# Three result transfers move from ScalarE's queue to GpSimd's, and ten blank products open the program in place of fourteen

## The chip, the core and the metric

The kernel runs on one core of one Trainium2 chip. The metric is device microseconds (us) of one execution, and less is better. A core has five engines with a queue of their own each, which run in order: TensorE (PE; its weight loads are listed apart as PEld), VectorE (DVE), ScalarE (ACT), GpSimd (POOL) and SyncE (SP). ACT, POOL and SP also start transfers (DMA). An instruction that waits for a semaphore holds up everything behind it in its queue.

## What is computed

An mLSTM cell over 768 steps for 4 batches x 8 heads of dimension 40, and behind it a feed-forward block with g = h - tanh(h):

```python
def _attn_ref(q, k, v, i_gate, f_gate, o_gate):
    ...
    for t in range(S):
        m_new = np.maximum(f_gate[:, :, t] + m, i_gate[:, :, t])
        f_stab = np.exp(f_gate[:, :, t] + m - m_new)
        i_stab = np.exp(i_gate[:, :, t] - m_new)
        C = f_stab[..., None, None] * C + i_stab[..., None, None] * np.einsum('bhd,bhe->bhde', vt, kt)
        n = f_stab[..., None] * n + i_stab[..., None] * kt
        h_tilde = np.einsum('bhde,bhe->bhd', C, qt)
        denom = np.maximum(np.abs(np.einsum('bhd,bhd->bh', n, qt)[:, :, None]), 1.0)
        y[:, :, t] = h_tilde / denom / (1.0 + np.exp(-o_gate[:, :, t]))

x = attn_out.transpose(0, 2, 1, 3).reshape(3072, 320)
h = x @ w_in                    # 320 x 2048
out = (h - np.tanh(h)) @ w_out  # 2048 x 320
```

## The kernel before

**Tiles.** The sequence is cut into chunks of 128 steps. A unit is one chunk of one batch (24 units), a group is two units, so 256 rows of x (12 groups). The 2048 hidden columns are eight pairs of 256, numbered p = 0 to 7. An item is one or two pairs of one group: it makes h ("up", tile `ph_up`), shrinks it to g (tile `gt`) and multiplies by `w_out` ("down", tiles `po` or `pS`).

**Two phases.** The first six units, the conversion of the weights and the first pairs of groups 0 to 2 are laid out by a small planner (`Plan`, lines 157 to 267). It keeps a time for each engine, and where TensorE would have nothing to do it puts in blank products (`awake`, line 428, or `stream`): matmuls of a constant, whose results nobody reads. `idle` (line 1704) decides how many. From about 107 us on a loop (line 1759) places the rest. There both products of an item are made with seven block products in place of eight, which needs sums of blocks: of x and of w_in (tiles `sums_in` and `part`, made on POOL in `sum_w_in`), of w_out (`wT`, POOL) and of g (`s`, DVE).

**The up product of the second phase** (`up_in_seven`, line 1227) has three stages in two PSUM banks. In stage three the sum lands in bank half b; ACT copies it to e (the last `COPY ph_up<-ph_up` of an item), and only then may PE add the last products to b. In the profile that is the group `ph_up<-xT,w_in` of 20 (4 of 128x128 and 16 quarters). Behind it PE has the attention products of a unit (`pT`, `pc`) and the down products of the item before (`pS`). DVE then adds (`both`), cubes and multiplies (`gt`), and PE's first up product of the next item has to wait until the cubes have read the banks.

**Groups 0 to 2.** Their first pairs were done in the planned phase and their sums lie in `part0` to `part2` in SBUF. Their last four pairs are done as two items each at the start of the loop, groups 0, 1, 2 in turn. When the last of them is done, `put_together` (line 1073) gathers the banks into the tile `ob` on DVE; later on DVE `add_parts` (line 1092) adds the stored sums, and `ob` is sent to `out`. The tile `part0` to `part2` is used again behind that: `sum_w_in` writes block sums of w_in for p = 0, 1, 2 into it on POOL.

**What sets the order.** Each engine's instructions are pinned in the order in which the code is run. `Clock.later(key, wait, step)` (line 141) puts a step off until an estimated clock has moved on by `wait`: `add_parts` comes 6.0 behind the gathering, and the transfer 1.0 behind `add_parts`. Whatever the loop emits in between stands between them on its engine.

Of the kernel before, what the change touches and what calls it, by code (L numbers as in the profile page):

```python
# [79 lines left out]
def kernel(  # L80
# [33 lines left out]
    V, A, SP, G = Pinned(nc.vector), Pinned(nc.scalar), Pinned(nc.sync), Pinned(nc.gpsimd)  # L114
# [42 lines left out]
    class Plan:  # L157
# [45 lines left out]
        def flow(cls, moved):  # L203
# [22 lines left out]
            return ends  # L226

        def run(self, idle, fill):
            while self.todo:
                ready = [(t, op) for op in self.todo if (t := self.start(op)) is not None]  # L230
# [23 lines left out]
                if op["engine"] == "T":  # L254
                    n = idle(self.free["T"], t)
                    self.done.append((t - n, t, 1.0))
                    us = us * (self.COLD[1] if t < self.COLD[0] else 1.0) + self.TURN * (op["tiles"] != self.tiles)
                    self.tiles = op["tiles"]
                    self.done.append((t, t + us, op["dense"]))
# [168 lines left out]
    def awake(n):  # L428

        if not spare:  # L430
            spare.append(ps_o.tile([128, 512], FP, name="awake", tag="po1"))
        stream(spare[0], n)

    def stream(bank, n):
        for _ in range(n):
            T.matmul(bank.rearrange("p (h t) -> p h t", h=HH), diag[:, 0], diag[:, 0:1].to_broadcast([128, HH, L]), start=True, stop=True)
# [636 lines left out]
    def put_together(g):  # L1073
        bank = pS[g]

        ob = mlp.tile([128, 5, HM], FP, name="ob", tag="ob")
        a = mlp.tile([128, HM], FP, name="a", tag="a", bufs=1)
        u = mlp.tile([128, 2, HM], FP, name="u", tag="u", bufs=1)

        def twice(t):  # L1080
            return t.unsqueeze(1).to_broadcast([128, 2, HM])

        def rest():
            V.tensor_tensor(out=ob[:, 0:5:4], in0=bank[0][:, 0:2], in1=twice(a), op=OP.add)
            V.tensor_tensor(out=u, in0=bank[1], in1=twice(ob[:, 4]), op=OP.add)
            V.tensor_tensor(out=ob[:, 3], in0=bank[1][:, 0], in1=u[:, 1], op=OP.add)
            V.tensor_tensor(out=ob[:, 1:3], in0=bank[2], in1=u, op=OP.add)
            c, b = divmod(g * GT, B)
            rows = out.rearrange("(b c t) n -> c t b n", b=B, c=NT)[c][:, b:b + GT]
            whole = ob[:, 0:4].rearrange("p (t two) n -> p t (two n)", two=2)  # L1090

            def add_parts():
                both = ob[:, 0:2 * GT]
                V.tensor_tensor(out=both, in0=both, in1=parts_of[g].rearrange("p t (two n) -> p (t two) n", two=2), op=OP.add)
                Clock.later("sent", 1.0, lambda: A.dma_start(out=rows, in_=whole))

            if g < FIRST:
                Clock.later("sent", 6.0, add_parts)
            else:
                Clock.later("sent", 2.0, lambda: A.dma_start(out=rows, in_=whole))  # L1100

        if g in third:
            return lambda: A.copy(out=a, in_=bank[0][:, 2]), rest
        A.copy(out=a, in_=bank[0][:, 2])
        Clock.later("result", 0.5, rest)
# [321 lines left out]
    plan = Plan(small=("b0", "b1"), a=1, up=1, po0=1, po1=1, gt=2, z=1, s4=1, P=4, vs=4, w64a=2, w64b=2, w=2, wm=2, ob=2)  # L1427
# [45 lines left out]
    of_tokens, of_states, exponentials, rows = {}, {}, [], []  # L1473
# [230 lines left out]
    def idle(t0, t1, share=0.9):  # L1704


        one = 0.43 if t0 < plan.COLD[0] else 0.217
        n = int((t1 - t0) * (1.0 if t0 < plan.COLD[0] else share if t0 > 18.0 or share == 1.0 else 0.65) / one)
        if n and not busy:
            awake(n + 4 if t0 < plan.COLD[0] else n)  # L1710
        else:
            pool, tag = next(((pool, tag) for name, pool, tag in (("a", ps_a, "a0"), ("up", ps_h, "ph0"), ("po0", ps_o, "po0"), ("po1", ps_o, "po1"))
                              if plan.tokens[name] and plan.tokens[name][0][0] <= t0), (None, None))
            if n and pool:
                stream(pool.tile([128, 512], FP, name="awake", tag=tag), n)
            else:
                n = 0
        return n * one

    plan.run(idle, lambda t0, t1: idle(t0, max(t1, t0 + 0.25), 1.0))  # L1720


# [280 lines left out]
```

## Time and profile before

| | |
|---|---|
| median of 3 runs | 495.69 us (495.55 to 496.15) |
| profiled execution, its own time | 496.64 us |
| profiled execution, span from first to last instruction | 494.9 us |
| mean granted clock of TensorE | 0.994 |
| PE idle in the whole span | 11.4 us (494.9 less 483.5 busy) |
| transfers `out<-ob` of 320 KB, started by ACT | 11, issue 0.36 to 0.44 us each |

The page gives the busy time of each engine, the share of each in the chain of work that ended last, and groups of instructions by tile. Times in the rows of the timeline are start and length; "[x <-Y]" behind a row says that the engine was idle for x us before it, and what ended that by the profile. Where TensorE is busy nearly all the time, its few idle stretches are the place to look.

### The profile page before, as it was taken

Reading aid. Unit: us, or ns where it says so; the run is one execution under the profiler, and the core shown is the slowest. Engines: PE = TensorE matmul, PEld = TensorE weight load, DVE = VectorE, ACT = ScalarE, POOL = GpSimd, SP = SyncE. Lnnn points to the kernel's source line nnn. Section 1 sums busy time; section 2 is a strip of 40 time slices with the busy share of each in tenths; the row PEclk is TensorE's granted clock in tenths of the full one; section 3 lists DMA queues with packets and bytes.
Section 4 is the critical chain, followed back from the end, with each engine's and each line's share of the span. In section 5 each row is a group of like instructions: output and inputs, shape, how many; then the busy total and the mean of one; then the engine's idle time right before and its main releaser. Section 6 shows DMA issues by size and latency. Waiting matters only on the chain.

```text
span 494.9 us, 13827 instructions
## 1 busy us (share of the span) xinstructions
PE 483.5 (98%) x5212; PEld 434.8 (88%) x5212; DVE 411.6 (83%) x966; ACT 268.9 (54%) x729; POOL 125.7 (25%) x248
## 2 busy tenths in 40 slices
PE   9999999999899989999999999999999999999995
PEld 5778877789798989999999999999999999898985
DVE  4899989998988988888888888888887988885853
ACT  4888978544344544554554454464455464454540
POOL 5642325826431522102112102102102102102000
PEclk9999999999989999999999999999999999999998
DMA  7995485223634435345445354454344343320001
GB/s 226 294 259 187 75 164 159 74 50 89 141 81 118 81 94 126 77 106 109 96 107 110 75 120 103 81 124 101 66 115 103 65 115 60 59 56 17 28 2 32
DMA packets 140076, 51.26 MB, mean 104 GB/s; under 512 B 119908, under 2 KB 132388, under 8 KB 140004
## 3 DMA queue, kind: packets, MB, share of 16 engines
q1 hardware_dynamic: 131084, 31.18, 30.8%
q0 software_dynamic: 5440, 15.05, 10.7%
q10 hardware_dynamic: 3480, 4.10, 2.4%
q8 instruction: 43, 0.70, 0.6%
q14 instruction: 29, 0.24, 0.2%
HBM read 38.40 MB, written 11.60 MB: 101 GB/s over the span
## 4 chain that ended last, share of the span: by engine, by line
PE 88%; DVE 4%; DMA 2%; SPq 1%; ACT 1%; issue 1%; POOL 0%; ACTq 0%; DVEq 0%
PE ph_up L129 38%; PE pS L129 30%; PE po L129 5%; PE pT L129 4%; PE ps L129 3%; PE pc L129 2%; PE awake L129 2%; PE ph L129 2%; SPq L106 1%; DMA z_in<-h_rows 1%; DVE gt L106 1%; DVE s L106 1%; DMA h_rows<-zt 1%; DVE ob L106 1%; ACT z L106 1%
## 5 line engine op out<-in xcount | busy, mean ns | idle before, releaser
L129 PE MATMUL ph_up<-xT,w_in 64*64 64x256 f32 (+3 forms) x1324 | 155.7, 350 | 4.4 <-ACT ph_up L106 3.3
L129 PEld LDWEIGHTS ph_up<-xT,w_in 128*128 128x128 f32 (+2 forms) x1324 | 114.1, 162 | 22.0 <-issue 4.7
L106 ACT COPY ph_up<-ph_up 128x256 f32<-128x256 f32 x117 | 41.8, 357 | 100.6 <-PE ph_up L129 60.5
L106 ACT ACTIVATE z<-ph_up 128x256 f32<-128x256 f32 (+1 forms) x98 | 40.6, 416 | 93.0 <-PE ph_up L129 88.4
L106 POOL DMA_DIRECT2D xT<-y_rows x54 | 31.6, 590 | 224.5 <-DMA y_rows<-yt 205.6
L129 PE MATMUL pS<-wT,s 128*128 128x160 f32 x504 | 86.7, 300 | 0.0
L129 PEld LDWEIGHTS pS<-wT,s 128*128 128x128 f32 x504 | 72.9, 191 | 0.3 <-issue 0.3
L106 ACT ACTIVATE q<-z,tiny 128x512 f32<-128x512 f32 (+1 forms) x98 | 68.9, 713 | 2.5
L106 DVE SCALAR_TENSOR_TENSOR gt<-q,gt 128x512 f32<-128x512 f32 (+1 forms) x98 | 66.0, 681 | 3.7 <-ACT q L106 1.1
L106 DVE TENSOR_TENSOR both<-ph_up,cs 128x256 f32<-128x256 f32 x78 | 32.7, 423 | 36.0 <-PE ph_up L129 31.4
L129 PE MATMUL pS<-w_out,gt 128*128 128x160 f32 x336 | 56.9, 312 | 0.0
L129 PE MATMUL ph_up<-xT,sums_in 128*128 128x128 f32 x336 | 51.6, 276 | 0.5 <-DVE gt L106 0.5
L129 PEld LDWEIGHTS pS<-w_out,gt 128*128 128x128 f32 x336 | 46.8, 190 | 4.4 <-issue 1.9
L129 PEld LDWEIGHTS ph_up<-xT,sums_in 128*128 128x128 f32 x336 | 45.5, 191 | 1.3 <-issue 0.7
L129 PE MATMUL ph_up<-xT,part 128*128 128x128 f32 x288 | 44.8, 278 | 0.0
L106 DVE SCALAR_TENSOR_TENSOR gt<-ph_up,z 128x256 f32<-128x256 f32 (+1 forms) x98 | 41.2, 459 | 2.3 <-ACT z L106 2.2
L129 PEld LDWEIGHTS ph_up<-xT,part 128*128 128x128 f32 x288 | 38.9, 191 | 1.7 <-ACT ph_up L106 1.7
L106 DVE TENSOR_TENSOR s<-gt 128x256 f32<-128x256 f32 x84 | 32.8, 431 | 1.4
L129 PE MATMUL pS<-wT,gt 128*128 128x160 f32 x168 | 29.8, 300 | 0.0
L129 PE MATMUL pS<-w_out,s 128*128 128x160 f32 x168 | 29.7, 299 | 0.0
L129 PE MATMUL po<-w_out,gt 128*128 128x320 f32 x96 | 27.9, 439 | 0.0
L106 DVE SCALAR_TENSOR_TENSOR gt<-both,z 128x512 f32<-128x512 f32 x39 | 27.0, 692 | 0.0
(141 smaller groups left out, 745.7 us busy)
## 6 DMA issues: line engine op xcount, KB each, us to landing
w<-in_moe_w_out POOLq DMA_DIRECT2D x8, 640.0 KB, 5.9
h_rows<-zt SPq DMA_DIRECT2D x68, 64.0 KB
z_in<-h_rows SPq DMA_DIRECT2D x68, 64.0 KB
w<-in_moe_w_in POOLq DMA_DIRECT2D x16, 256.0 KB, 6.0
kz<-in_kT SPq DMA_DIRECT2D x48, 80.0 KB
o<-in_o_gate SPq DMA_DIRECT2D x24, 160.0 KB
qz<-in_qT SPq DMA_DIRECT2D x44, 80.0 KB
out<-ob ACTq DMA_DIRECT2D x11, 320.0 KB
```

What stands on the lines that cost most here:

```text
L106: i = method(*args, **kwargs)
L129: return cls.keep(nc.tensor.matmul(*args, **kwargs))
```

## The change

Two lines are edited:

```diff
             def add_parts():
                 both = ob[:, 0:2 * GT]
                 V.tensor_tensor(out=both, in0=both, in1=parts_of[g].rearrange("p t (two n) -> p (t two) n", two=2), op=OP.add)
-                Clock.later("sent", 1.0, lambda: A.dma_start(out=rows, in_=whole))
+                G.dma_start(out=rows, in_=whole)
...
         if n and not busy:
-            awake(n + 4 if t0 < plan.COLD[0] else n)
+            awake(n)
```

The transfers of groups 0, 1 and 2 are started by POOL, and no longer put off. The planner's numbers are as they were; the first call of `awake` now makes 10 blank products, and the four that go are the last four ahead of the first transposes on PE (`gate<-ident,w_in`). No other instruction of PE, DVE or SP changes its place.

On ACT, in the item behind the end of group 0 (`cs` is a copy of half a bank, `z` and `q` are the first steps of the shrinking), these rows stood:

```order
144 L106 COPY ph_up<-ph_up 128x256
145 L106 COPY cs<-ph_up 128x256
146 L106 COPY ph_up<-ph_up 128x256
147 L106 DMA out<-ob 128x2x320
148 L106 COPY ph_up<-ph_up 128x256
```

and now these:

```order
144 L106 COPY ph_up<-ph_up 128x256
145 L106 COPY cs<-ph_up 128x256
146 L106 COPY ph_up<-ph_up 128x256 x2
147 L106 ACTIVATE z,sums<-ph_up 128x256 x2
148 L106 ACTIVATE q<-z,tiny 128x512
```

The transfer stood ahead of the last copy of the item, the one that lets PE go on; now nothing stands between the two copies. The same holds at the ends of groups 1 and 2.

On POOL, at the same place, the rows now are (`part_145` is the tile of group 0's sums, used again for w_in's; `xT` is x of a later group, fetched through `y_rows` in DRAM):

```order
83 L106 MEMSET k 128x40
84 L106 MEMSET vs 128x23
85 L106 DMA out<-ob 128x2x320
86 L106 TENSOR_TENSOR part_145<-w_in 128x2x128
87 L106 TENSOR_TENSOR part_145<-w_in,part_145 128x128 x2
88 L106 DMA xT_90<-y_rows 64x3x128
```

Row 85 is new, and the rest has moved down by one. Row 86 had to wait for the same addition on DVE before, since it overwrites the tile that the addition reads. At group 2 it is:

```order
110 L106 TENSOR_TENSOR wT<-w_out 128x160
111 L106 TENSOR_TENSOR wT<-w_out,wT 128x160
112 L106 DMA out<-ob 128x2x320
113 L106 TENSOR_TENSOR part_147<-w_in 128x2x128
114 L106 TENSOR_TENSOR part_147<-w_in,part_147 128x128 x2
115 L106 DMA xT_91<-y_rows 64x3x128
```

Again only the transfer (row 112) is new.

## The prediction

> **What bounds the kernel.** I read the page's busy times first, then the list of who waited for whom on PE.
>
> ```profile
> PE 483.5 (98%) x5212; PEld 434.8 (88%) x5212; DVE 411.6 (83%) x966; ACT 268.9 (54%) x729; POOL 125.7 (25%) x248
> PE 88%; DVE 4%; DMA 2%; SPq 1%; ACT 1%; issue 1%; POOL 0%; ACTq 0%; DVEq 0%
> PE ph_up L129 <- ACT ph_up L106: 3.3, 2, 1.8
> PE ph_up L129 <- POOL part L106: 1.0, 1, 1.0
> ```
>
> PE is busy for 98% of the span and makes 88% of the chain that ended last. The two lines of waits (us in total, times, longest) are three gaps of 4.3 us together, and no other line of that list behind PE's start has more than 0.5. So the time is PE's work plus these few gaps, and the question is which gaps go. The timeline shows the first of the three, at the end of group 0:
>
> ```profile
> 133.11 0.61 PE L129 MATMUL ph_up<-xT,w_in 128*128 128x128 f32 x4
> 133.56 0.61 PE L129 MATMUL ph_up<-xT,sums_in 128*128 128x128 f32 x4
> 134.18 0.82 DVE L106 TENSOR_TENSOR ob<-ob,part 128x640 f32<-128x640 f32 x1
> 135.03 0.44 ACTq L106 DMA_DIRECT2D out<-ob  x1
> 135.51 0.36 ACT L106 COPY ph_up<-ph_up 128x256 f32<-128x256 f32 x1 [3.06 <-DVE o L106]
> 135.92 2.15 PE L129 MATMUL ph_up<-xT,w_in 128*128 128x128 f32 x20 [1.76 <-ACT ph_up L106]
> ```
>
> Read from below: PE waits for ACT's copy, the copy stands behind the issue of the transfer, and the issue behind DVE's addition, which ends at 135.00. ACT itself had been idle for 3.06 us. The other two are alike:
>
> ```profile
> 156.06 0.61 PE L129 MATMUL ph_up<-xT,part 128*128 128x128 f32 x4
> 157.22 0.36 ACT L106 COPY ph_up<-ph_up 128x256 f32<-128x256 f32 x1 [2.26 <-DVE o L106]
> 157.72 1.71 PE L129 MATMUL ph_up<-xT,w_in 128*128 128x128 f32 x20 [1.05 <-POOL part L106]
> ...
> 176.23 0.61 PE L129 MATMUL ph_up<-xT,sums_in 128*128 128x128 f32 x4
> 178.41 1.74 PE L129 MATMUL ph_up<-xT,w_in 128*128 128x128 f32 x20 [1.57 <-ACT ph_up L106]
> ```
>
> The second is put down to POOL's `part`. I take it for a coincidence: these products read no `part` tile, and ACT's copy ends 0.14 us ahead of them, at 157.58.
>
> **The change, part by part. 1. The transfers leave ACT.** The copy then needs only PE's product that stands two groups ahead, so it is done before PE asks for it. Groups of four such products follow each other in 0.45 us (133.11 to 133.56), so PE's 20 products could start at 133.56 + 0.45 = 134.01 and not 135.92: 1.91 us. At the second place it is 157.72 - 156.51 = 1.21, at the third 178.41 - 176.68 = 1.73. Together 4.85.
>
> The first gap cost more than its length:
>
> ```profile
> 137.00:138.00 1.00, 1.00 (x18) 0.56 0.06 16
> 138.00:139.00 1.00, 1.00 (x28) 0.50 0.27 40
> 139.00:140.00 1.00, 1.00 (x32) 0.50 0.24 38
> 180.00:181.00 1.00, 1.00 (x48) 1.00 0.23 39
> 140.89 1.35 PE L129 MATMUL pS<-w_out,gt 128*128 128x160 f32 x8
> 161.06 1.35 PE L129 MATMUL pS<-w_out,gt 128*128 128x160 f32 x8
> ```
>
> The column behind PE's busy time is the granted clock. It falls to half at 137 behind the first gap, for some 3 us, and stays at 1.00 behind the third. From the 20 products to the next `pS` PE takes 140.89 - 135.92 = 4.97 us there, and 161.06 - 157.72 = 3.34 at the second place: 1.6 us lost. Without the gap this goes too. PE's lead at 140.89 is then 1.91 + 1.6 = 3.5 us.
>
> The Trainium skill, TensorE: Matmul & The Clock Gate, "What's actually happening", says that the clock is halved after a window of about 3.4 us with too little work, and that the windows run free of the kernel. The trace agrees with the length; by that rule the 1.6 us would be in some executions and not in others, which is the first rival below.
>
> **2. What DVE takes back.** PE cannot keep the whole lead, since DVE is nearly full in this stretch. DVE gains only where it was idle for want of PE:
>
> ```profile
> 138.17 0.96 DVE L106 TENSOR_TENSOR both<-ph_up,cs 128x256 f32<-128x256 f32 x2 [0.90 <-PE ph_up L129]
> 146.44 0.49 DVE L106 TENSOR_TENSOR ob<-pS,a 128x320 f32<-128x320 f32 x1 [0.49 <-ACT a L106]
> 149.37 0.42 DVE L106 TENSOR_TENSOR both<-ph_up,cs 128x256 f32<-128x256 f32 x1 [0.76 <-PE ph_up L129]
> 150.32 0.75 DVE L106 SCALAR_TENSOR_TENSOR gt<-ph_up,z 128x256 f32<-128x256 f32 x2
> 152.20 0.61 PE L129 MATMUL ph_up<-xT,part 128*128 128x128 f32 x4
> 159.54 0.96 DVE L106 TENSOR_TENSOR both<-ph_up,cs 128x256 f32<-128x256 f32 x2 [0.55 <-PE ph_up L129]
> 171.15 0.74 DVE L106 SCALAR_TENSOR_TENSOR gt<-ph_up,z 128x256 f32<-128x256 f32 x2
> 172.37 0.61 PE L129 MATMUL ph_up<-xT,sums_in 128*128 128x128 f32 x4
> 190.11 0.96 DVE L106 TENSOR_TENSOR both<-ph_up,cs 128x256 f32<-128x256 f32 x2 [1.32 <-PE ph_up L129]
> ```
>
> The rule is that PE's first up product of an item comes behind the two cubes (`gt<-ph_up,z`) of the item before. DVE's lead by 150.32 is 0.90 + 0.49 + 0.76, say 2.1. The cubes then end at 151.07 - 2.1 = 148.97, and PE, which with its 3.5 would be there at 148.70, starts at 149.0: its lead falls to 3.2. The second place adds 1.21: 4.4. DVE has 2.1 + 0.55 = 2.65 by then. In the item that ends group 2 the cubes end at 171.89 - 2.65 = 169.24, and PE would be there at 172.37 - 4.4 = 167.97. It waits 1.3 us, and its lead falls to 3.1. The third place adds 1.73: **4.8 us**. Behind it DVE gains 1.32 more at 190.11, and the groups from 3 on have no additions of parts, so I let nothing be lost there.
>
> Bounds for this term: if DVE gained nothing at all before 172.37, PE's lead there could be 172.37 - 171.89 = 0.5, and with 1.73 it ends at 2.2. If DVE took nothing back it would be 4.85 + 1.6 = 6.45. The 4.8 follows the rows step by step, so I take it.
>
> **3. The issue on POOL.** The trace has no transfer of `ob` by POOL; the nearest are others that POOL starts:
>
> ```profile
> L106 POOL DMA_DIRECT2D xT<-y_rows x54: 534/612/642, 131.1 to 445.5; - x54
> L106 POOL DMA_DIRECT2D w<-in_moe_w_out x8: 722/736/751, 7.8 to 78.9; - x8
> 177.69 0.84 POOL L106 TENSOR_TENSOR part<-w_in 128x256 f32<-128x256 f32 x1 [7.48 <-DVE ob L106]
> 178.60 1.05 POOL L106 TENSOR_TENSOR part<-w_in,part 128x128 f32<-128x128 f32 x2
> 184.05 0.61 PE L129 MATMUL ph_up<-xT,part 128*128 128x128 f32 x4
> ```
>
> An issue takes 0.53 to 0.75 us of POOL; I take 0.74, from the one with the same shape of rows (128x2x320). POOL waited for the same addition before, so no wait is new, and `part` comes 0.74 later. Queued behind are `part` and the `xT` transfers, which wait for `y_rows` anyway. The tightest user is the last: PE reads group 2's `part` at 184.05, with its lead at 179.25. POOL's wait for the addition would end at 177.69 - 2.65 = 175.0, and it is done with issue and sums (177.69 to 179.65, so 0.74 + 1.96) at 177.7. So 1.5 us are left and the cost is nothing; without that cover it would be up to 0.74.
>
> **4. Four blank products fewer.**
>
> ```profile
> 4.05 1.18 PEld L129 LDWEIGHTS <-diag 128*128 128x128 bf16 x6 [0.23 <-issue]
> 5.05 0.41 DVE L106 TENSOR_TENSOR w_out<-w_out,w_in 32x256 f32<-32x256 f32 x1
> 5.66 0.20 PEld L133 LDWEIGHTS gate<-ident,w_in 32*128 32x128 f32 x2 [0.42 <-issue]
> 21.91 0.49 DVE L106 TENSOR_SCALAR w_e<-w 128x640 int32<-128x640 int32 x1 [0.40 <-DMA w<-in_moe_w_in]
> ```
>
> The fast ones follow each other in 1.18 / 6 = 0.2 us, so PE is free 0.8 us earlier. But the second transposes need DVE's row of 5.05, which ends at 5.46, so the work behind them gains some 0.2 (5.66 less 5.46). At 21.91 DVE waits for the weights' transfer, which no PE work starts, and a lead from the start ends there. I take 0. Ends: -0.8 if all of it survived; +1.6 if PE, now idle for some 0.4 us and then on short products, lost the clock once as it did at 137.
>
> **The sum.** 4.8 + 0 + 0 off the profiled execution's 496.64 gives **491.8 us**. The median, 495.69, lies 0.95 under the profiled execution. Two readings: the recording costs that, and the timed runs lose the clock as well, then it is 495.69 - 4.8 = 490.9; or they don't lose it. In that case the old program would reach the second place 1.6 us sooner, with DVE as sooner, so the gain is 4.8 - 1.6 = 3.2 and the time 492.5. 491.8 lies between them and I keep it.
>
> **The rivals.**
> - *No clock loss in the timed runs*: 492.5, as just worked out. For it speaks that the second and third gap (1.05 and 1.57 us) show none, so 1.76 is near the edge. It lies inside my forecast, which I give as 490.6 to 493.2: 0.74.
> - *DVE holds PE throughout*: a lead of 2.2 or less, 493.4 to 494.5. For it: DVE is idle at little more than the rows shown, and the units' transfers through DRAM could arrive no sooner. Against it: the third gap stands behind the last gathering, and goes whole. 0.13.
> - *The clock at the start*: 1.6 us on top, 492.5 to 494.1. For it: ahead of 5.46 PE would have little but two short transposes. Against it: at 178.41 PE had been idle for 1.57 us and kept its clock. 0.08.
> - *The edit does nothing* (PE waits for `part` at all three places, as the profile writes at the second): 495.7. Against it: the tiles that these products read. 0.03.
> - *Slower*: POOL's issue is long. If the third one took 0.74 + 1.5 = 2.2 us, PE would start to wait for `part` at 184.05; with the lead of 4.8 it would be slower beyond 7.0 us an issue. All 54 + 8 issues above lie under 0.76, against it. 0.02, 496.5 and above.
>
> The Trainium skill, DMA: Bandwidth & Descriptors, "SWDGE vs HWDGE vs iDMA", speaks against the change: plain transfers belong to SP or ACT, since GpSimd computes its descriptors in software and DVE can lock it out of the memory that it writes them to. By that rule POOL's issue could stretch as in the last rival; the issue rows above, made beside a busy DVE, show nothing of it.
>
> **How the numbers follow.** The range 490.6 to 493.5 takes in both readings and most of the start's bound. A measurement of this kernel can tell about 0.2% (1.0 us) from no change. Faster by more than that: the forecast, the start and nearly all of the second rival, 0.93; within it 0.05; slower 0.02.
>
> **What would show it.** In the profile after, the 20 products at the three places have no wait for ACT; the granted clock stays at 1.00 there; PE has new waits for DVE's `gt` near 149 and 167 to 169, some 1.6 us together; POOL's three issues take about 0.74 each. I am wrong if PE waits for `part`, if the clock falls between 5 and 12 us, or if the gaps go and come back whole as waits for DVE behind 180.

## The result, and the profile after

| | before | changed |
|---|---|---|
| median, 20 runs each | 495.98 us | 491.52 us |
| lowest to highest | 494.94 to 497.81 us | 491.00 to 497.14 us |
| mean | 495.99 us | 493.21 us |

The ratio of the times is 0.9944, with a 95% interval from 0.9917 to 0.997. The prediction, 491.8 us with a range from 490.6 to 493.5, holds the median. It does not hold the runs: they lie in two clusters, 13 from 491.0 to 491.8 and 7 from 496.4 to 497.1, with nothing between. The upper cluster was not foreseen at this price: its rival, "the clock at the start", had 492.5 to 494.1. The profiled execution, at 496.5 us, is one of the seven, so its profile shows both what the change gained and what it lost.

First lines of the page and, from the list of who waited for whom on PE, two lines of the kernel after (us in total, times, longest):

```profile
span 494.8 us, 13817 instructions
PE 486.8 (98%) x5208; PEld 435.5 (88%) x5208; DVE 411.2 (83%) x966; ACT 268.9 (54%) x729; POOL 127.2 (26%) x251
PE ph_up L129 <- DVE gt L106: 1.3, 3, 0.7
PE pS L129 <- DVE ob L106: 0.3, 1, 0.3
```

The two lines of before that made 4.3 us (waits for ACT's copy and, by the list, for POOL's `part`) are gone. Yet the span is that of before, 494.8 against 494.9, and PE is busy for 486.8 us where it was 483.5, with four instructions fewer. PE took longer for the same work somewhere. The timeline at the end of group 0 shows the gain:

```profile
138.13 0.36 ACT L106 COPY ph_up<-ph_up 128x256 f32<-128x256 f32 x1 [0.86 <-PE ph_up L129]
138.37 0.61 PE L129 MATMUL ph_up<-xT,sums_in 128*128 128x128 f32 x4
138.82 1.63 PE L129 MATMUL ph_up<-xT,w_in 128*128 128x128 f32 x20
138.99 0.82 DVE L106 TENSOR_TENSOR ob<-ob,part 128x640 f32<-128x640 f32 x1
140.10 0.74 POOL L106 DMA_DIRECT2D out<-ob  x1 [2.17 <-DVE ob L106]
...
158.33 1.64 PE L129 MATMUL ph_up<-xT,w_in 128*128 128x128 f32 x20
159.55 0.74 POOL L106 DMA_DIRECT2D out<-ob  x1 [7.84 <-DVE ob L106]
160.31 0.92 POOL L106 TENSOR_TENSOR part<-w_in 128x256 f32<-128x256 f32 x1
178.84 0.61 PE L129 MATMUL ph_up<-xT,w_in 128*128 128x128 f32 x4
```

ACT's copy is done by 138.49, ahead of DVE's addition, and the 20 products follow the four before them after 0.45 us. At the second place they start at 158.33, ahead of POOL's `part` at 160.31, so `part` was indeed never what they waited for. But all of this comes late: the group at 138.37 stood at 133.56 before. The timeline of PE's first 19 us shows where the 4.8 us went (three rows of before, then those of after):

```profile
6.02 1.16 PE L129 MATMUL ps<-qz,kz 40*128 40x128 f32 x16
7.59 1.24 PE L129 MATMUL awake<-diag 128*128 128x512 bf16 x5
11.98 1.88 PE L129 MATMUL ph<-vs,P 128*128 128x41 f32 x16
```

```profile
5.52 0.42 PE L133 MATMUL gate<-ident,w_in 32*128 32x32 f32 x2
6.08 2.08 PE L129 MATMUL ps<-qz,kz 40*128 40x128 f32 x16
8.97 2.34 PE L129 MATMUL awake<-diag 128*128 128x512 bf16 x5
13.25 3.86 PE L129 MATMUL awake<-diag 128*128 128x512 bf16 x9
16.94 1.88 PE L129 MATMUL ph<-vs,P 128*128 128x41 f32 x16
```

The same 16 products take 2.08 us and not 1.16, the same 5 blank ones 2.34 and not 1.24, and so on up to 16.8 us. Only the group at 16.94 has its old length. In this execution TensorE never left the half clock with which it starts until then, while before it left it at 4.05 (in the prediction's rows, the six weight loads at 0.2 us). The granted clock is of no help here:

```profile
14.00:16.00 2.00, 2.00 (x6) 0.76 (x5) 0.00 (x0) 1.97 (x5) 1.99 (x4) 1.00 0.73 268
```

This window of after has 1.00 in the column behind the engines' busy times, though the six blank products in it follow each other at 0.43 us, where six of the prediction's rows take 0.2 each. The trace's own record of the clock begins only at the rise, here at 16.82 us, and the column shows 1.00 for the time ahead of it. There the clock has to be told from the distances.

### The profile page after: what moved, and what is told of

The parts are those of the page before. It is cut to its first block, busy times and chain, and to the rows that moved or that the text cites. A ratio compares the mean times of both kernels' runs of the same rounds, so it can differ in the third digit from the quotient of the medians.

```text
span 494.8 us, 13817 instructions
## 1 busy us (share of the span) xinstructions
PE 486.8 (98%) x5208; PEld 435.5 (88%) x5208; DVE 411.2 (83%) x966; ACT 268.9 (54%) x729; POOL 127.2 (26%) x251
## 4 chain that ended last, share of the span: by engine, by line
PE 89%; DVE 6%; issue 1%; ACT 1%; DMA 1%; SPq 1%; DVEq 0%; ACTq 0%
PE ph_up L129 38%; PE pS L129 30%; PE po L129 5%; PE ps L129 4%; PE pT L129 4%; PE awake L129 3%; PE pc L129 2%; PE ph L129 2%; DVE gt L106 1%; DVE s L106 1%; DVE ob L106 1%; SPq L106 1%; ACT z L106 1%; DVE ys L106 1%; DVE zt L106 1%
```

## The experiments

Two theories stood against each other. A: the ten blank products make the clusters, and the transfers gain about 4.6 us in every run. B: the transfers on POOL make the clusters.

**Each part alone, more blank products, and ACT's queue behind the copy.** The four kernels are:

```diff
 e1: transfers on GpSimd, but
+            awake(n + 4 if t0 < plan.COLD[0] else n)
 e2: the kernel before, but
+            awake(n)
 e3: transfers on GpSimd, but
+            awake(n + 8 if t0 < plan.COLD[0] else n)
 e4: the kernel before, but
+                Clock.later("sent", 2.0, lambda: A.dma_start(out=rows, in_=whole))
```

> The transfers on GpSimd, but fourteen blank products at the first as before. Theory A (the changed kernel's two clusters of times come from its ten blank products: where TensorE's clock does not rise during them, it stays low until about 16 us and the program is 5 us late; the transfers themselves are worth 4.6): one cluster near 491.3, no run above 494, and in the profile fast blank products from about 4 us. Rival B (the two clusters come from the transfers on GpSimd): two clusters, 491.3 and 496.5, the upper with about a third of the runs. Rival C (the good cluster of the changed kernel owes something to the earlier start): one cluster at 492 or above.

> The kernel before with ten blank products in place of fourteen; the transfers stay on ScalarE. Theory A: two clusters, about 495.9 with some two thirds of the runs and about 501 with a third. Rival B: one cluster near 495.9. Rival C: a lower cluster clearly under 495.9, by as much as e1 lies above 491.3.

> The transfers on GpSimd and eighteen blank products at the first. Theory A: fourteen are enough, so one cluster; four more fast products of 0.2 us delay the start by 0.8, of which the wait of VectorE for the weights near 22 us should take up most: 491.3 to 492.1. If fourteen are not quite enough (some runs of e1 high), e3 has fewer of these than e1. Rival B: two clusters as in e1.

> The kernel before with its fourteen blank products and the three transfers on ScalarE, put off by 2.0 in place of 1.0, so that each stands behind the copy that lets TensorE go on and not ahead of it. Theory A (only the place ahead of the copy cost time, not ScalarE's queue): the same as e1, about 491.3, and no wait of the twenty products for ScalarE. Rival D (ScalarE's queue itself, its issue or what stands behind the transfer, costs as well, and GpSimd is the gain): 492.5 to 495, with waits for ScalarE left in the profile.

The runs of the kernel before on the same chip had a median of 495.68 (17 runs). All times below are in us; "upper" counts the runs that lie 4 us or more above the others of their kernel.

| | blank products | transfers | median (runs) | lowest to highest | upper | ratio, 95% interval |
|---|---|---|---|---|---|---|
| e1 | 14 | POOL | 491.77 (6) | 491.10 to 493.27 | 0 | 0.9927 (0.9911 to 0.9942) |
| e2 | 10 | ACT, ahead of the copy | 495.13 (12) | 494.41 to 500.06 | 1 | 0.9987 (0.9976 to 0.9998) |
| e3 | 18 | POOL | 492.46 (5) | 492.38 to 493.00 | 0 | 0.9936 (0.9924 to 0.9949) |
| e4 | 14 | ACT, behind the copy | 491.89 (5) | 491.55 to 492.53 | 0 | 0.9928 (0.9916 to 0.9941) |

A holds in all four: the upper cluster comes with ten blank products, with the transfers on either queue. Two of its numbers did not: e2 has 1 run of 12 in the upper cluster where a third was expected, and e1 is spread over 2.2 us. e4 is the same as e1, and its 20 products wait for nothing at the three places, so nothing of the gain is POOL's: it is enough that the transfer no longer stands ahead of the copy. Rival C has a small part of the truth: e2's lower runs, at a median of 495.06, are 0.6 under before. And e3 is 0.7 over e1, so a later start is not taken up by the wait of DVE near 22 us, against what was expected.

e2's profiled execution fell in its upper cluster, like that of after. The two differ by the transfers alone, so PE's timeline in them can be laid side by side. Rows of e2 (the waits have the names that they had before), and the window behind its first gap:

```profile
138.41 0.61 PE L129 MATMUL ph_up<-xT,sums_in 128*128 128x128 f32 x4
140.76 1.52 PE L129 MATMUL ph_up<-xT,w_in 128*128 128x128 f32 x16 [1.75 <-ACT ph_up L106]
158.41 0.61 PE L129 MATMUL ph_up<-xT,part 128*128 128x128 f32 x4
160.96 0.68 PE L129 MATMUL ph_up<-xT,w_in 128*128 128x128 f32 x4 [1.04 <-POOL part L106]
177.31 0.66 PE L129 MATMUL ph_up<-xT,sums_in 128*128 128x128 f32 x4
181.82 0.38 PE L129 MATMUL ph_up<-xT,w_in 128*128 128x128 f32 x1 [1.69 <-ACT ph_up L106]
```

```profile
141.00:145.00 4.00, 4.00 (x90) 3.51 (x90) 3.23 (x10) 2.28 (x8) 0.88 (x2) 1.00 0.34 93
```

and the two of after that are still missing for the pairs:

```profile
156.99 0.61 PE L129 MATMUL ph_up<-xT,part 128*128 128x128 f32 x4
176.13 0.71 PE L129 MATMUL ph_up<-xT,sums_in 128*128 128x128 f32 x4
```

The lead of after over e2 is 0.04 us ahead of the first place (138.41 less 138.37) and 1.94 behind it (140.76 less 138.82); 1.42 ahead of the second and 2.63 behind it; 1.18 ahead of the third and 2.98 behind it. So the places give 1.90, 1.21 and 1.80, and DVE takes back 0.5 and 1.45 between them. In e2 the gap of 1.75 cost no clock, as the window behind it shows (1.00): without that, the transfers are worth 3.0 us at the third place and 3.1 at PE's last product. The spans differ by more, 3.6. Behind PE's last product each of the twelve profiles has another 4.5 to 5.3 us, which do not follow the change (e1 4.5, e4 5.3).

**How many blank products, and who takes the lead back.**

```diff
 e5: the changed kernel, but
+            awake(n - 3 if t0 < plan.COLD[0] else n)
 e6: the changed kernel, but
+            awake(n + 2 if t0 < plan.COLD[0] else n)
 e7: e1, but in add_parts
-                V.tensor_tensor(out=both, in0=both, in1=parts_of[g]...
+                G.tensor_tensor(out=both, in0=both, in1=parts_of[g]...
```

> The changed kernel with seven blank products at the first in place of ten. Theory A (the clock rises at a moment that differs from run to run over some 3.4 us, seen at 4.05, 5.4 and 5.8 so far; where TensorE's blank products run out before, it misses the rise): at half clock seven products last until 1.14 + 7 x 0.43 = 4.1 us, so the clock must rise by then; the high cluster, near 496.5, holds over half of the runs (a quarter with ten, and 1.3 / 3.4 more). Low cluster 491.0 to 491.5. Rival E (the high cluster has nothing to do with how long the blank products last): about the same share as with ten, a quarter.

> The changed kernel with twelve blank products at the first. Theory A: they last until 6.3 us at half clock, beyond every rise seen so far, so few runs or none in the high cluster; the rest 491.0 to 491.8, about 0.2 under e1. Rival E: a quarter of the runs near 496.5.

> As e1 (transfers on GpSimd, fourteen blank products), and the three additions of the stored sums run on GpSimd too, ahead of their transfers. Theory A with VectorE taking back 1.3 us of TensorE's lead between 149 and 170 us because it has no idle time left there: VectorE has 3 x 0.82 us less to do, so TensorE's waits for the cubes shrink, by up to 1.3 us: 490.5 to 491.3. Rival F (the take-back comes from the gathering of the banks in the same item, which lies ahead of the cubes whatever VectorE did before): the waits stay, 491.5 to 492. If GpSimd's addition takes over 1.6 us longer than the spare time ahead of its sums, TensorE waits for them near 180 us: 492 and more.

> The changed kernel once more on the same chip as the other counts of blank products. Theory A: two clusters, 491.3 and 496.5, with a share in the upper one between those of seven and twelve. A profile from the lower cluster would show fast blank products ahead of 5.5 us and the same three places as e1.

The kernel before had 495.50 (23 runs) on this chip.

| | blank products | median (runs) | lowest to highest | above 494 | ratio, 95% interval |
|---|---|---|---|---|---|
| e5 | 7 | 494.17 (12) | 491.31 to 497.20 | 8 | 0.997 (0.9947 to 0.9994) |
| e6 | 12 | 492.19 (6) | 491.35 to 492.69 | 0 | 0.9923 (0.9905 to 0.9941) |
| e7 | 14 | 492.17 (6) | 491.67 to 493.01 | 0 | 0.9923 (0.9905 to 0.9942) |
| e8 | 10 | 491.65 (12) | 490.92 to 497.09 | 3 | 0.9931 (0.9905 to 0.9957) |

Eight of twelve with seven, three of twelve with ten, none of six with twelve: the share follows the number, against rival E. Two expectations were off. e6 is 0.4 above the 491.8 that was its upper end. And there are more than two clusters: four runs of e5 lie from 494.07 to 494.20 and four from 496.12 to 497.20. e8's profiled execution, at 494.67, is of the middle sort. Its PE rows, of which the last has nine blank products:

```profile
11.66 1.91 PE L129 MATMUL ps<-qz,kz 40*128 40x128 f32 x16
13.49 2.12 PE L129 MATMUL awake<-diag 128*128 128x512 bf16 x9
```

The nine take 2.12 us here, as before the change, and 3.86 in the profile after: the clock rose near 13 us (the trace's record begins at 13.25), 3.6 us sooner than there. Each chance that is missed costs another step.

e7 did not help. PE's waits for the cubes stay:

```profile
PE ph_up L129 <- DVE gt L106: 1.5, 3, 0.5
```

That is 1.5 us and not the 1.3 of e1, and one of the three, 0.51 us at 140.63, is new; so are two waits of 0.3 for other steps. But e7 did not relieve DVE. Rows of e1, then of e7, at the addition of group 0:

```profile
132.71 0.76 DVE L106 TENSOR_TENSOR s<-gt 128x256 f32<-128x256 f32 x2
```

```profile
132.72 2.54 DVE L106 TENSOR_TENSOR s<-gt 128x256 f32<-128x256 f32 x2
133.07 1.56 POOL L106 TENSOR_TENSOR ob<-ob,part 128x640 f32<-128x640 f32 x1
```

Beside POOL's addition, two of DVE's instructions take 2.54 us where they take 0.76 in e1. From 128 to 183 us DVE is busy for as long as in e1, with three instructions fewer (before, e1, e7; behind the length of the window the busy time of DVE):

```profile
128.00:183.00 55.00, 49.16 (x115) 0.97 0.47 109
128.00:183.00 55.00, 51.86 (x121) 1.00 0.47 109
128.00:183.00 55.00, 51.87 (x118) 1.00 0.47 109
```

So e7 does not decide between A and F.

**The gathering behind the cubes, and four blank products.**

```diff
 e9: e1, but
-                Clock.later("sent", 6.0, add_parts)
+                Clock.later("sent", 2.5, add_parts)
-        Clock.later("result", 0.5, rest)
+        Clock.later("result", 0.5 if g >= FIRST else 4.0, rest)
 e10: the changed kernel, but
+            awake(n - 6 if t0 < plan.COLD[0] else n)
```

> As e1, but VectorE gathers the banks of groups 0 to 2 only behind the cubes of the next item (four instructions, 2.2 us, moved behind six others of 2.7 us); the addition of the stored sums then stands a few instructions earlier than in e1. Rival F, as e7 left it (the take-back of 1.3 us is the gathering, which stands ahead of the cubes that TensorE waits for): TensorE's waits for the cubes at the ends of the three groups go, and waits for the gathered banks (down products that need the banks free) come in their place, each up to 2.5 us where e1 has 0.3 or none: 492.5 to 498. If VectorE's load as a whole were the reason, the sum of its waits would stay as in e1 and the time between 491.5 and 492.5.

> The changed kernel with four blank products at the first. Theory A, sharpened: the clock rises only at the end of a window of 3.41 us that is filled with products for some 2.75 us; the seven products of e5 (2.8 of a window from 1.54 to 4.95) were enough, and four (1.7 us) cannot be, wherever the window falls: no run of the low cluster, all above 493.5, in steps near 494.2 and 496.5. If the rise only has a chance that falls with the number of products, some runs in ten still lie near 491.5.

Before had 496.21 here (17 runs). e9 had 500.54 (6 runs, 499.36 to 503.08; ratio 1.0096, 1.0068 to 1.0123). e10 had 495.19 (12 runs, 493.58 to 497.34; ratio 0.998, 0.9964 to 0.9996), with six runs from 493.6 to 494.5, six from 495.9 to 497.3, and none in the lower cluster, as expected. PE's only wait of note behind the start in e9, and a window behind its first gap:

```profile
PE pS L129 <- DVE ob L106: 7.8, 3, 2.7
```

```profile
133.00:134.00 1.00, 1.00 (x5) 1.00 (x5) 0.93 (x4) 0.00 (x0) 1.00 (x5) 0.50 0.81 205
```

The list has no wait for the cubes any more, and three for the gathered banks in their place, up to 2.7 us each. That is what F expected, and it shows that the gathering's place decides which of DVE's steps PE waits for. It does not show that DVE's load is beside the point: with 51.86 of 55 us busy, as in e1, DVE has little to spare, and whichever of the two steps stands first, the other comes later. The time is above F's range. The gaps also cost the clock (0.50 in the eighth column; by the trace's record from 129.1 to 135.9 and from 176.8 to 180.3), which the expectation had left out.

## Why the prediction was right, and where it was not

**The transfers leave ACT: right, to a few hundredths.** 1.91, 1.21 and 1.73 us were forecast for the three places. 1.90, 1.21 and 1.80 came. The products had no wait for ACT, and `part` was a coincidence.

**The half clock behind the first gap: a term of some runs only.** The forecast put 1.6 us for it into the sum, named the reading without it (a gain of 3.2), and kept 491.8 because it lay between the two readings. The reading without it was right where the clock held: 3.0 to 3.1 in the pair of e2 and after. The other exists too: of the 23 runs of before beside e5, the five with a mean granted clock of 0.993 or 0.994 have a median of 497.08, the twelve at 0.999 or more one of 495.4, which is 1.7 less. The profiled 496.64, from which the sum set out, was of the former. By the medians the transfers gained 3.9 (495.68 to 491.77 in e1). With six runs of e1 spread over 2.2 us it is not known closer than that. The prediction took 1.76 us to be near the edge of the length that costs the clock. Length alone does not decide: 1.76 us cost it in before, and 1.75 us in e2 did not.

**What DVE takes back: right, and for the reason given.** 0.3 and 1.3 us were forecast, 0.5 and 1.45 came in the pair. The whole chain of the sum can be followed in e1 too, against the profile of before, which lost the clock. e1's rows at the steps that the prediction named:

```profile
133.69 0.61 PE L129 MATMUL ph_up<-xT,sums_in 128*128 128x128 f32 x4
137.41 1.35 PE L129 MATMUL pS<-w_out,gt 128*128 128x160 f32 x8
148.18 0.74 DVE L106 SCALAR_TENSOR_TENSOR gt<-ph_up,z 128x256 f32<-128x256 f32 x2
149.06 0.68 PE L129 MATMUL ph_up<-xT,part 128*128 128x128 f32 x4 [0.18 <-DVE gt L106]
153.65 1.63 PE L129 MATMUL ph_up<-xT,w_in 128*128 128x128 f32 x20
168.77 0.74 DVE L106 SCALAR_TENSOR_TENSOR gt<-ph_up,z 128x256 f32<-128x256 f32 x2
169.65 0.68 PE L129 MATMUL ph_up<-xT,sums_in 128*128 128x128 f32 x4 [0.68 <-DVE gt L106]
174.17 1.63 PE L129 MATMUL ph_up<-xT,w_in 128*128 128x128 f32 x20
```

Ahead of the first place e1 is 0.13 us later than before (133.69 less 133.56). With that added, PE's lead is 3.6 us at `pS`, then 3.3, 4.2, 2.9 and 4.4, where 3.5, 3.2, 4.4, 3.1 and 4.8 were forecast. DVE's cubes come 2.3 and 2.5 us sooner, where 2.1 and 2.65 were forecast. So DVE had little more to give than its idle stretches in the prediction's rows: without the gaps it is busy for 94% of the stretch from 128 to 183 us. The gathering of the banks is a part of what stands ahead of the cubes there (e9). The new waits are smaller than the 1.6 us that were named: 0.9 for the cubes, since 0.5 of the 1.3 in the list stood in before too, and 0.3 for `ob`. The rest of what is taken back is no wait in the list.

**The issue on POOL: right.** Three issues of 0.74 us each, as taken from `w<-in_moe_w_out`. The spare time at group 2, forecast as 1.5 us, in the profile after:

```profile
180.12 0.74 POOL L106 DMA_DIRECT2D out<-ob  x1 [7.62 <-DVE ob L106]
181.89 0.99 POOL L106 TENSOR_TENSOR part<-w_in,part 128x128 f32<-128x128 f32 x2
184.38 0.61 PE L129 MATMUL ph_up<-xT,part 128*128 128x128 f32 x4
```

`part` is done at 182.88 and read at 184.38, so 1.5 us are left. The rule of the Trainium skill, DMA: Bandwidth & Descriptors, "SWDGE vs HWDGE vs iDMA", which spoke against GpSimd, cost nothing here: e1 and e4 are 0.1 us apart.

**Four blank products fewer: this step failed, in both directions.** It was costed at nothing.
- The gain was denied because DVE's wait for the weights at 21.91 would end any lead. It doesn't. In e3 PE's transposes start at 7.38 and in e1 at 6.33; in the item that ends group 0, at 130.72 and 129.62, the 1.05 us are all still there, and the spans differ by 1.3. The wait at 21.91 belonged to one execution: in no other profile does this row wait, and in e5, whose transposes start at 5.50, it comes at 20.95. (In before itself most of such a lead was gone later: its transposes, at 5.66, are 0.67 us ahead of e1's, its row at 133.56 only 0.13.) So the lower cluster has 0.5 to 0.6 more than the transfers give, by the medians: 491.31 against 491.77 in e1, and 495.06 in e2 against 495.68.
- The loss was the rival "the clock at the start", with the right place, at 0.08 and 1.6 us. It came in 11 of 44 runs with ten products (7 of 20, 1 of 12, 3 of 12) and cost some 3 us when the clock rose near 13 us, and some 5 when it rose near 16.8. The price was that of one window of half clock. But the work right behind the transposes did not bring the clock up, so several windows in a row were lost. The reason given against it, that PE kept its clock over 1.57 us of idle time at 178.41, was about keeping a clock, not about getting one.

So the number was right in part by luck. For the transfers the sum was sound: its 4.8 (4.4 by the rows of e1) belongs to an execution that loses the clock at the first gap, it was taken off such an execution's own time, and 491.8 lies among e1's runs, whose median is 491.77. The luck is in the blank products. They moved 13 of 20 runs down by some 0.5 us and 7 of 20 up by some 5, and the median lies near the forecast because it falls into the lower cluster. In the mean the changed kernel is worse than the transfers alone, though these runs are too few to call it clear of noise: 493.21 (20 runs) and 492.68 (12 runs, e8) against 491.98 for e1, and on the chip of e8 twelve blank products had 492.10. The version to keep is e1 or e4: the gain of the transfers, with fourteen blank products and no upper cluster.

## What to carry to other kernels

Look for instructions that wait (a transfer's issue behind an addition) ahead of ones that another engine needs: moving the first behind the second gives the gap as read from the timeline, on either queue. That the profiled execution had its clock early does not make warm-up products spare: ask how long they must last for the worst moment of the rise, and time enough runs to see two clusters. Where a gap goes, add up how much sooner the next engine in the chain can come, from its own idle stretches: the lead beyond that is lost. And an experiment that moves work off an engine has to be read in that engine's busy time first; in e7 it had not changed.

## What the runs showed that was not expected

**When the clock rises.** The first weight loads of the blank products at full clock, 0.2 us from each other, in e3 and e4; behind those of each a window of 1 us at the end, with the granted clock in the eighth column:

```profile
5.78 1.18 PEld L129 LDWEIGHTS <-diag 128*128 128x128 bf16 x6 [0.25 <-issue]
```

```profile
490.00:491.00 1.00, 0.00 (x0) 0.00 (x0) 0.00 (x0) 0.00 (x0) 0.00 (x0) 0.71 0.04 16
```

```profile
4.51 0.96 PEld L129 LDWEIGHTS <-diag 128*128 128x128 bf16 x5 [0.26 <-issue]
```

```profile
489.00:490.00 1.00, 0.00 (x0) 0.00 (x0) 0.00 (x0) 0.00 (x0) 0.00 (x0) 0.59 0.00 0
```

The rise comes near 5.8 and 4.5, and at 4.05 in before; the traces' records of the clock begin at 5.74, 4.49 and 4.00, and at 5.35 in e1. e3 and e4 show a fall as well, when PE has finished: at 0.71 and 0.59 of a window of 1 us the clock was half for 0.58 and 0.82 us, so it fell at 490.42 and 489.18. Both times 484.6 to 484.7 us lie between rise and fall, 142 times 3.413. So the clock moves on a grid of 3.41 us that has another phase in each execution. The Trainium skill, TensorE: Matmul & The Clock Gate, "Part 1: The HAM clock gate", has a free-running window of 3413 ns; these runs agree with it.

**How full such a stretch has to be.** In e5 the seven products last from 1.14 to 4.31, and its transposes at 5.50 already run at full clock:

```profile
1.14 3.17 PE L129 MATMUL awake<-diag 128*128 128x512 bf16 x7 [1.14 <-DVE probe L106]
5.50 0.28 PE L133 MATMUL gate<-ident,w_in 32*128 32x32 f32 x2 [1.20 <-DVE w_in L106]
```

```profile
489.00:490.00 1.00, 0.00 (x0) 0.00 (x0) 0.00 (x0) 0.00 (x0) 0.00 (x0) 0.82 0.05 16
```

Its clock rose while PE was idle (the trace's record begins at 4.96). It fell at 489.64 (0.82 in the last row), and 142 steps of 3.413 us ahead of that is 4.97: the stretch of 3.41 us that ends there holds PE's products from 1.56 to 4.31, 2.75 us. Four products, 1.7 us, were never enough in e10. Suppose that 2.75 us are needed. Then the moment of the rise has to lie between 1.14 + 2.75 and the products' end + 3.41 - 2.75. This estimate from the rows gives 31% of the phases for seven products (end 4.3), 69% for ten (5.6) and 94% for twelve (6.4). Seen were 4 of 12, 33 of 44 and 6 of 6 runs. The profiles of the upper runs fit it. Their records begin at 16.82 (after), 17.12 (e2) and 13.25 (e8), and whole steps of 3.413 ahead of that there was a moment at 6.58, 6.88 and 6.43, all beyond 5.6 + 3.41 - 2.75 = 6.26. The stretches that ended there were filled, but only 2.4, 2.1 and 2.5 us of them with blank products; transposes and products of 40 rows made up the rest, and the clock did not rise. Such products are not worth nothing: in e8 the stretch that ended at 13.25 had 1.8 us of blank products and 1.6 of the products of 40 rows, and it was enough. How much they count, so that PE can look busy there for 8 us without its clock rising, was not tried.
